# The last unit of a retention and mixture-of-adapters kernel: small products moved between engines, its copies reordered, its stores regrouped

## The chip, the cores and the metric

The kernel runs on one core of a Trainium2 chip. The metric is the device time of one execution in microseconds; runs are compared by their medians.

## The reference

Two stages, the second fed by the first. Retention over 8 batches, 8 heads, 576 positions and head dimension 64; then, for each of the 4608 tokens (512 numbers each), a mixture of 8 adapters of rank 16, of which the best two by a gate are added to the token.

```python
scores = scale * np.matmul(q, k.transpose(0, 1, 3, 2))
ret = scores * Dmat[None, :, :, :]          # Dmat: gamma_h ** (i - j) where i >= j, else 0
attn_out = np.matmul(ret, v)
x = attn_out.transpose(0, 2, 1, 3).reshape(B * S, H * D)
logits = x @ w_gate
# the two largest logits of each token, softmax over these two -> w
delta[mask] += w[mask, k, None] * (z @ B[e])   # z = x[mask] @ A[e]
return x + delta
```

## The kernel before, in words

The sequence is cut into chunks of 128 positions, and a unit is one chunk of two batches. The last 64 positions of the sequence are half a chunk, so there a unit takes four batches: rows 0 to 63 of a tile belong to two batches, rows 64 to 127 to the next two. These are the units NU-2 and NU-1, the last two of all. In their output tiles the column index `b` (0 or 1) and the row half `t` (0 or 1) together name the batch, `4*bp + 2*t + b`.

Per unit: queries and keys are scaled and transposed (`stage_T`), scores are made (`stage_S`), masked on DVE, and multiplied with the values and the running state (`stage_X`, PSUM tile `px`). The result, already transposed, is copied to SBUF as `xT`. Logits and adapter inputs come out of one product (`stage_Z`, `pz`), 128 columns of adapter inputs and 8 gate logits. The gate works on these: the two largest (`max`), a threshold test (`ge`), a sigmoid on ACT (`sg`), their product on POOL (`cm`), and the weighted adapter inputs (`zc`), also on POOL. `zc` is transposed on PE (`pzt`), copied on ACT (`zT`), and multiplied with the second adapter matrix (`stage_Y`), which adds to a PSUM tile `po` into which `stage_B` has transposed `xT` back. `evict_o` copies `po` to `osb`, and `store` sends `osb` to memory.

The program order on each engine is the order in which the code is written (a manual schedule): nothing reorders it. `finish()` writes out the end by hand. There the last unit is split by column half `b`, and its tiles carry an `e`: `pze` and `ze` (logits), `nse`, `gee`, `sge`, `cme`, `zce`, `pzte`, `zTe`, `poe`, `oe`. In the order of before, `finish()` computes both `pze` halves (L714), then for each half the gate (L726 to L740), with the small step of unit NU-2 between them; then `stage_B`, `stage_Y`, `evict_o` and `store` of unit NU-2; then the transposes and output products of the last unit (`small_b`, `output_b`).

Stores of full chunks (L525) send 128 rows of 512 numbers of one batch, 256 KB in one piece of memory. The two units of half chunks store each batch by itself, 64 rows, 128 KB in one piece of memory (L530 for unit NU-2, of which two on POOL's queue; L776 for the last unit, of which one on ACT's queue).

Of the kernel before, what the change touches and what calls it, by code (L numbers as in the profile page):

```python
# [10 lines left out]
FP32 = mybir.dt.float32  # L11
FP16 = mybir.dt.float16

ALU = mybir.AluOpType
AFT = mybir.ActivationFunctionType
# [3 lines left out]
def kernel(  # L19
# [10 lines left out]
    nc = tc.nc  # L30
    B, H, S, Dh = q.shape
    Ntok, Dm = out.shape
    E = moe_w_gate.shape[1]
    R = moe_A.shape[2]
    ER = E * R
    HP = H // 2
# [9 lines left out]
    scale = 1.0 / float(np.sqrt(Dh))  # L46
# [34 lines left out]
    mo = ctx.enter_context(tc.tile_pool(name="moe", bufs=2))  # L81
    pp = ctx.enter_context(tc.tile_pool(name="pp", bufs=1, space=bass.MemoryType.PSUM))
# [6 lines left out]
    ident16 = cpool.tile([128, 128], FP16, tag="ident16", name="ident16", align_bytes=256)  # L89
# [4 lines left out]
    id64 = pack[:, 0:64]  # L94
# [12 lines left out]
    NU = len(units)  # L107
# [267 lines left out]
    def stage_P(u, tag="x1"):  # L375
        pzt = pp.tile([128, 2, 128], FP16, tag=tag, name="pzt")
        for b in range(2):
            nc.tensor.matmul(
                pzt[:, b, :], lhsT=st[u]["zc"][:, b, :], rhs=ident16,
                is_transpose=True, start=True, stop=True,  # L380
            )
        st[u]["pzt"] = pzt

    def evict_z(u):
        zt = mo.tile([128, 2, 128], FP16, tag="zT", name="zT")
        nc.scalar.copy(out=zt, in_=st[u]["pzt"])
        st[u]["zT"] = zt
# [82 lines left out]
    def stage_Y(u):  # L470
        s = st[u]
        bv = Bcat.rearrange("p (a o d) -> p a o d", a=HP, o=2)
        for ho in range(2):
            for b in range(2):
                nc.tensor.matmul(  # L475
                    s["po"][ho][:, b, :, :],
                    lhsT=s["zT"][:, b, :],
                    rhs=bv[:, :, ho, :],
                    start=False,
                    stop=True,  # L480
                    skip_group_check=True,
                )

    def evict_o(u, engines=(nc.scalar, nc.scalar)):
        s = st[u]
        s["osb"] = mo.tile(
            [128, 2, HP, 2, 64], FP32, tag="osb", name="osb", bufs=3, align_bytes=256
        )
        for ho in range(2):
            eng = engines[ho]  # L490
            copy = eng.copy if eng is nc.scalar else eng.tensor_copy
            copy(out=s["osb"][:, :, :, ho, :], in_=s["po"][ho])  # L492
# [23 lines left out]
            )  # L516

    o3 = out.rearrange("(b s) m -> b s m", s=S)

    def store(u):  # L520
        c, bp = units[u]
        of = st.pop(u)["osb"].rearrange("p b a o d -> p b (a o d)")
        for b in range(2):
            if c < NFULL:
                nc.sync.dma_start(  # L525
                    out=o3[2 * bp + b, 128 * c : 128 * c + 128, :], in_=of[:, b]
                )
            else:
                for t in range(2):
                    (nc.gpsimd if b and u == NU - 2 else nc.sync).dma_start(  # L530
                        out=o3[4 * bp + 2 * t + b, 128 * c : 128 * c + 64, :],
                        in_=of[64 * t : 64 * t + 64, b],
                    )


    def load_batch(u, w, b):
        c, bp = units[u]
# [17 lines left out]
    for dt in range(HP):  # L555
        nc.sync.dma_start(  # L556
            out=AW[:, dt, 0:ER].rearrange("p (e r) -> p e r", e=E),
# [96 lines left out]
    def back(u):  # L654
        if has(u):
            stage_B(u)
# [6 lines left out]
    def small(u, tag="x1"):  # L663
        if has(u):
            stage_P(u, tag)
            evict_z(u)
# [26 lines left out]
    def finish():  # L693
        u = NU - 1
        s = st[u]
        store(u - 3)
        routing_4(u - 2)
        scores(u)
        logits(u - 1)
        small(u - 2)  # L700
        back(u - 2)
        choose(u - 1)
        routing_3(u - 1)
        output(u - 2)
        routing_4(u - 1)
        products(u)
        store(u - 2)

        bv = Bcat.rearrange("p (a o d) -> p a o d", a=HP, o=2)
        pz, zs, zc, po, osb = [], [], [], [], []  # L710
        for b in range(2):
            pz.append(pp.tile([128, ER + E], FP32, tag=f"u{b}", name="pze"))
            for dt in range(HP):
                nc.tensor.matmul(  # L714
                    pz[b], lhsT=s["xT"][b][:, dt, :], rhs=AW[:, dt, :],
                    start=(dt == 0), stop=(dt == HP - 1), skip_group_check=True,
                )
        for b in range(2):
            z = mo.tile([128, ER + E], FP32, tag=f"ze{b}", name="ze", bufs=1)
            m8 = mo.tile([128, E], FP32, tag=f"m8e{b}", name="m8e", bufs=1)  # L720
            ns = mo.tile([128, 1], FP32, tag=f"nse{b}", name="nse", bufs=1)
            ge = mo.tile([128, E], FP32, tag=f"gee{b}", name="gee", bufs=1)
            sg = mo.tile([128, E], FP32, tag=f"sge{b}", name="sge", bufs=1)
            cm = mo.tile([128, E], FP32, tag=f"cme{b}", name="cme", bufs=1)
            c = mo.tile([128, ER], FP16, tag=f"zce{b}", name="zce", bufs=1)
            nc.scalar.copy(out=z, in_=pz[b])  # L726
            nc.vector.max(out=m8, in_=z[:, ER : ER + E])
            nc.vector.scalar_tensor_tensor(
                out=ns, in0=m8[:, 0:1], scalar=-1.0, in1=m8[:, 1:2],
                op0=ALU.mult, op1=ALU.subtract,  # L730
            )
            nc.vector.tensor_tensor(
                out=ge, in0=z[:, ER : ER + E],
                in1=m8[:, 1:2].broadcast_to((128, E)), op=ALU.is_ge,
            )
            nc.scalar.activation(
                out=sg, in_=z[:, ER : ER + E], func=AFT.Sigmoid, bias=ns, scale=2.0
            )
            nc.gpsimd.tensor_tensor(out=cm, in0=ge, in1=sg, op=ALU.mult)
            nc.gpsimd.tensor_tensor(  # L740
                out=c.rearrange("p (e r) -> p e r", e=E),
                in0=z[:, 0:ER].rearrange("p (e r) -> p e r", e=E),
                in1=cm.unsqueeze(2).broadcast_to((128, E, R)),
                op=ALU.mult,
            )
            zc.append(c)
            if b == 0:
                small(u - 1, "x0")
        back(u - 1)
        stage_Y(u - 1)  # L750
        evict_o(u - 1, (nc.scalar, nc.vector))
        store(u - 1)

        def small_b(b):
            p = pp.tile([128, 128], FP16, tag=f"u{b}", name="pzte")
            nc.tensor.matmul(
                p, lhsT=zc[b], rhs=ident16, is_transpose=True, start=True, stop=True
            )
            zt = mo.tile([128, 128], FP16, tag=f"zTe{b}", name="zTe", bufs=1)
            nc.scalar.copy(out=zt, in_=p)  # L760
            return zt

        def output_b(b, zt):
            o = mo.tile([128, HP, 2, 64], FP32, tag=f"oe{b}", name="oe", bufs=1, align_bytes=256)
            for ho, eng in ((0, nc.scalar), (1, nc.vector)):
                nc.tensor.matmul(
                    po[b][ho], lhsT=zt, rhs=bv[:, :, ho, :],
                    start=False, stop=True, skip_group_check=True,
                )
                (eng.copy if eng is nc.scalar else eng.tensor_copy)(  # L770
                    out=o[:, :, ho, :], in_=po[b][ho]
                )
            c, qd = units[u]
            of = o.rearrange("p a o d -> p (a o d)")
            for t in range(2):
                (nc.scalar if b and t else nc.sync).dma_start(  # L776
                    out=o3[4 * qd + 2 * t + b, 128 * c : 128 * c + 64, :],
                    in_=of[64 * t : 64 * t + 64],
                )

        zt0 = small_b(0)
        for b, tag in ((0, "s"), (1, "x")):
            po.append(
                [pp.tile([128, HP, 64], FP32, tag=f"{tag}{ho}", name="poe") for ho in range(2)]
            )
            for dt in range(HP):
                for ho in range(2):
                    sl = slice(64 * ho, 64 * ho + 64)
                    nc.tensor.matmul(
                        po[b][ho][:, dt, :], lhsT=s["xT"][b][sl, dt, :], rhs=id64[sl, :],  # L790
                        is_transpose=True, start=(dt == 0), stop=False, skip_group_check=True,
                    )
        output_b(0, zt0)
        output_b(1, small_b(1))

    stage_A(2)
    logits(0)
# [103 lines left out]
```

## Time and profile before

| | us |
|---|---|
| median of 3 runs | 190.33 (190.16 to 191.59) |
| profiled execution, its time | 190.79 |
| profiled execution, its span | 188.9 |
| outside the span | 1.9 |

Engines are busy for these shares of the span: PE 89%, weight loads 79%, DVE 60%, ACT 60%, POOL 58%. Times in the timeline are microseconds from the span's start; a timeline line gives start, duration, engine, source line, operation, tiles written and read, the count, and the idle time before it with what ended it. In the DMA views, a slice digit is the mean busy share of the core's 16 DMA engines in tenths, and the line below it is the rate in GB/s. A DMA instruction on a queue (SPq, ACTq, or on POOL) is the issuing of a transfer; the transfer itself runs on the DMA engines afterwards.

### The profile page before, as it was taken

The page shows a single profiled execution, that of the slowest core. Times are in us where ns is not written, and L with a number is a line of the kernel's source. Part 1 is how long each engine was busy: PE and PEld are TensorE (multiplying, and loading weights), DVE is VectorE, ACT ScalarE, POOL GpSimd, SP SyncE. Part 2 cuts the span into 40 slices and gives each one's busy share as a digit, 9 for nine tenths or more (in the row PEclk, how much of TensorE's full clock was granted, in tenths as well). Part 3 has the DMA queues.
Part 4 walks back from the last instruction along what each step waited for, and adds up shares of the span by engine and source line. Part 5 has one row for each costly group of instructions (what it writes and reads, how often), then busy time and mean ns, then how long its engine had stood idle before and what let it go on. Part 6 is the DMA issues. An engine that isn't in the chain of part 4 may idle for free.

```text
span 188.9 us, 10441 instructions
## 1 busy us (share of the span) xinstructions
PE 167.3 (89%) x4675; PEld 148.9 (79%) x4675; DVE 113.3 (60%) x227; ACT 114.1 (60%) x255; POOL 108.7 (58%) x162
## 2 busy tenths in 40 slices
PE   3989598799889889898999999999997999999960
PEld 3578498588879788788999989899996988988840
DVE  1384837665296475748577787777594846555240
ACT  3437163735569484765767868494959394674650
POOL 1333321567769988493949586675969397520240
PEclk9999969999999999999999999999999999999998
DMA  7999969999999999999999999999998853112325
GB/s 157 248 221 225 227 70 232 202 224 246 224 228 235 262 252 277 252 260 247 241 257 246 266 232 250 221 278 226 271 206 243 181 169 115 50 68 111 115 56 166
DMA packets 108075, 38.99 MB, mean 206 GB/s; under 512 B 88768, under 2 KB 103488, under 8 KB 108032
## 3 DMA queue, kind: packets, MB, share of 16 engines
q1 hardware_dynamic: 107568, 37.71, 81.1%
q8 instruction: 36, 0.59, 1.4%
q0 software_dynamic: 240, 0.39, 1.0%
q10 hardware_dynamic: 224, 0.24, 0.5%
q14 instruction: 7, 0.06, 0.1%
HBM read 29.02 MB, written 9.44 MB: 204 GB/s over the span
## 4 chain that ended last, share of the span: by engine, by line
PE 59%; SPq 14%; issue 7%; DMA 6%; POOL 5%; DVE 4%; ACT 2%; POOLq 0%; ACTq 0%
PE px L350 15%; PE pz L393 12%; PE ps_s L269 8%; PE pu L300 6%; PE po L475 5%; PE po L459 4%; PE pt_k L215 4%; SPq L148 3%; SPq L556 3%; PE pt_q L202 3%; DMA k<-in_k_dram 3%; SPq L160 3%; DMA q<-in_q_dram 3%; POOL k L179 2%; SPq L538 2%
## 5 line engine op out<-in xcount | busy, mean ns | idle before, releaser
L179 POOL TENSOR_TENSOR k<-k,pack 128x512 f32<-128x512 f32 x32 | 34.9, 1109 | 17.4 <-DMA k<-in_k_dram 16.5
L350 PE MATMUL px<-x,v 128*64 128x64 f32 (+1 forms) x576 | 39.3, 226 | 2.6 <-DVE x L289 0.8
L289 DVE TENSOR_TENSOR x<-ps_s,pack 64x512 f32<-64x512 f32 (+1 forms) x38 | 25.1, 660 | 25.9 <-PE ps_s L269 25.6
L350 PE MATMUL px<-qT,v 128*64 128x64 f32 (+1 forms) x576 | 39.2, 226 | 1.3 <-DVE qT L289 1.1
L350 PEld LDWEIGHTS px<-x,v 128*64 128x64 f32 (+1 forms) x576 | 36.2, 140 | 4.4 <-ACT kT L240 1.0
L350 PEld LDWEIGHTS px<-qT,v 128*64 128x64 f32 (+1 forms) x576 | 36.1, 140 | 1.9 <-DVE qT L289 1.2
L393 PE MATMUL pz<-AW,xT 128*128 128x136 f32 x272 | 36.1, 286 | 0.6 <-ACT kT L240 0.6
L393 PEld LDWEIGHTS pz<-AW,xT 128*128 128x128 f32 x272 | 32.6, 190 | 1.8 <-ACT kT L240 0.8
L169 POOL TENSOR_TENSOR qs<-q,pack 128x512 f32<-128x512 f32 x25 | 26.1, 1062 | 4.1 <-DMA q<-in_q_dram 4.1
L406 ACT COPY zs<-pz 128x272 f32<-128x272 f32 x17 | 6.6, 386 | 33.2 <-PE pz L393 32.5
L289 DVE TENSOR_TENSOR qT<-ps_s,pack 64x512 f32<-64x512 f32 (+1 forms) x38 | 25.1, 660 | 1.1
L269 PE MATMUL ps_s<-qT,kT 64*64 64x64 f32 x1152 | 23.6, 224 | 2.1 <-issue 1.4
L269 PEld LDWEIGHTS ps_s<-qT,kT 64*64 64x64 f32 x1152 | 20.4, 137 | 6.2 <-issue 3.1
L441 POOL TENSOR_TENSOR cm<-ge,sg 128x16 f32<-128x16 f32 x17 | 4.0, 234 | 36.5 <-PE pt_k L215 16.9
L316 POOL COPY v<-SP 64x512 f32<-64x512 f32 x32 | 20.5, 640 | 1.6
L300 PE MATMUL pu<-v,k 64*64 64x64 f32 x1024 | 19.2, 221 | 0.8 <-DMA v<-in_v_dram 0.8
L240 ACT COPY kT<-pt_k 128x512 f32<-128x512 f32 x34 | 18.2, 589 | 1.2 <-PE pt_k L215 1.0
L253 DVE COPY x<-qT 64x512 f32<-64x512 f32 x17 | 14.5, 852 | 7.4 <-ACT qT L235 5.0
L366 ACT COPY xT<-px 128x512 f32<-128x512 f32 x28 | 16.3, 625 | 4.4 <-PE px L350 4.4
L300 PEld LDWEIGHTS pu<-v,k 64*64 64x64 f32 x1024 | 16.9, 134 | 2.5 <-DMA v<-in_v_dram 0.9
L492 ACT COPY osb<-po 128x512 f32<-128x512 f32 x33 | 17.6, 584 | 1.0 <-PE po L475 1.0
L252 DVE COPY x<-qT 64x512 f32<-64x512 f32 x14 | 8.1, 579 | 16.0 <-ACT qT L235 12.0
(68 smaller groups left out, 242.6 us busy)
## 6 DMA issues: line engine op xcount, KB each, us to landing
v<-in_v_dram SPq DMA_DIRECT2D x36, 256.0 KB, 5.2
q<-in_q_dram SPq DMA_DIRECT2D x34, 256.0 KB, 5.2
out_dram<-osb SPq DMA_DIRECT2D x32, 256.0 KB, 4.2
k<-in_k_dram SPq DMA_DIRECT2D x15, 512.0 KB, 5.7
k<-in_k_dram SPq DMA_DIRECT2D x6, 256.0 KB, 4.3
q<-in_q_dram SPq DMA_DIRECT2D x1, 512.0 KB, 6.9
out_dram<-oe SPq DMA_DIRECT2D x3, 128.0 KB, 3.3
AW<-in_moe_A_dram SPq DMA_DIRECT2D x4, 64.0 KB, 3.6
```

Of the source, the lines that this page charges most:

```text
L169: engines[b].tensor_tensor(out=qs[:, :, 4 * b : 4 * b + 4, :].rearrange("p e h d -> p h e d"), in0=tl[:, b * H : b * H + H, :].rearrange(" ...
L179: engines[b].tensor_tensor(out=tl[:, b * H : b * H + H, :], in0=tl[:, b * H : b * H + H, :], in1=g[:, c, :].unsqueeze(2).broadcast_to((128 ...
L240: nc.scalar.copy(out=tl[:, r], in_=st[u]["p" + w][r])
L253: eng.tensor_copy(out=x2[0:64, 1, b], in_=qT[64:128, 1, b])
L269: nc.tensor.matmul(ps[ho][64 * t : 64 * t + 64, b, hp, :], lhsT=kT[sl, t, b, hp, :], rhs=qT[sl, t, b, hp, :], start=(hp == 0 and b == bs[0 ...
L289: nc.vector.tensor_tensor(out=out, in0=in0, in1=m, op=ALU.mult)
L300: nc.tensor.matmul(pu[t][64 * ho : 64 * ho + 64, b, hp, :], lhsT=kn[sl, h, :], rhs=block(u, t)[sl, h, :], start=(hp == 0 and b == 0), stop ...
L316: copy(out=dst[:, :, :, ho, :], in_=src[64 * ho : 64 * ho + 64])
L350: nc.tensor.matmul(px[b][64 * ho : 64 * ho + 64, hp, t, :], lhsT=block(u, t)[rw, b * H + 2 * hp + ho, :], rhs=facing(u, t, ho)[rw, b, hp, ...
L366: nc.scalar.copy(out=xt.rearrange("p a (t i e) -> p (a t) e i", t=2, e=2), in_=px.rearrange("p a t (e i) -> p (a t) e i", e=2),)
L393: nc.tensor.matmul(pz[:, b, :], lhsT=st[u]["xT"][b][:, dt, :], rhs=AW[:, dt, :], start=(dt == 0), stop=(dt == HP - 1), skip_group_check=True,)
L492: copy(out=s["osb"][:, :, :, ho, :], in_=s["po"][ho])
```

## The change

Only `finish()` and the branch of `store` that serves the half chunks are touched.

1. In the last unit, `cm` and `zc` are computed on DVE in place of POOL.
2. The last unit's second logits copy (`ze` of half 1) and its `max`, `nse`, `gee` are issued ahead of unit NU-2's `zT` copy.
3. `stage_B` of the last unit's half 0 comes before `stage_Y` of unit NU-2; the last unit's output copies are all on ACT; both output copies of unit NU-2 go to DVE, behind the last unit's second `zc`; the store of unit NU-2 is issued after the last unit's first store.
4. Each column half `b` of these two units is stored as one transfer from 128 partitions. In memory it is two runs of 64 rows, one for each batch `t`, with other batches between them. The store of unit NU-2 is two transfers on SP; the last unit's first is on SP, its second on ACT.

```diff
     o3 = out.rearrange("(b s) m -> b s m", s=S)
+    o5 = out.rearrange("(g t b s) m -> g b t s m", t=2, b=2, s=S)
...
             else:
-                for t in range(2):
-                    (nc.gpsimd if b and u == NU - 2 else nc.sync).dma_start(
-                        out=o3[4 * bp + 2 * t + b, 128 * c : 128 * c + 64, :],
-                        in_=of[64 * t : 64 * t + 64, b],
-                    )
-
+                nc.sync.dma_start(
+                    out=o5[bp, b, :, 128 * c : 128 * c + 64, :], in_=of[:, b]
+                )
...
+        def choose_b(b):
+            z, m8 = small_tile("ze", b, ER + E), small_tile("m8e", b, E)
+            ns, ge = small_tile("nse", b, 1), small_tile("gee", b, E)
             nc.scalar.copy(out=z, in_=pz[b])
             nc.vector.max(out=m8, in_=z[:, ER : ER + E])
...
+        def sigmoid_b(b):
+            sg = small_tile("sge", b, E)
             nc.scalar.activation(
-                out=sg, in_=z[:, ER : ER + E], func=AFT.Sigmoid, bias=ns, scale=2.0
-            )
-            nc.gpsimd.tensor_tensor(out=cm, in0=ge, in1=sg, op=ALU.mult)
-            nc.gpsimd.tensor_tensor(
+                out=sg, in_=ze[b][:, ER : ER + E], func=AFT.Sigmoid, bias=nse[b], scale=2.0
+            )
...
+        def weigh_b(b):
+            cm, c = small_tile("cme", b, E), small_tile("zce", b, ER, FP16)
+            nc.vector.tensor_tensor(out=cm, in0=gee[b], in1=sge[b], op=ALU.mult)
+            nc.vector.tensor_tensor(
                 out=c.rearrange("p (e r) -> p e r", e=E),
...
             p = pp.tile([128, 128], FP16, tag=f"u{b}", name="pzte")
...
+            zt = small_tile("zTe", b, 128, FP16)
             nc.scalar.copy(out=zt, in_=p)
             return zt
...
+        def back_b(b, tag):
...
+        def output_b(b, zt, engines):
...
+            (nc.scalar if b else nc.sync).dma_start(
+                out=o5[qd, b, :, 128 * c : 128 * c + 64, :],
+                in_=o.rearrange("p a o d -> p (a o d)"),
+            )
+
+        choose_b(0)
+        sigmoid_b(0)
+        stage_P(u - 1, "x0")
+        choose_b(1)
+        evict_z(u - 1)
+        back(u - 1)
+        back_b(0, "s")
+        zt0 = weigh_b(0)
+        stage_Y(u - 1)
+        sigmoid_b(1)
+        back_b(1, "x")
+        output_b(0, zt0, (nc.scalar, nc.scalar))
+        zt1 = weigh_b(1)
+        evict_o(u - 1, (nc.vector, nc.vector))
+        store(u - 1)
+        output_b(1, zt1, (nc.scalar, nc.scalar))
```

More of the change, by code (lines that the diff above doesn't have):

```diff
@@ L709, in finish @@
         bv = Bcat.rearrange("p (a o d) -> p a o d", a=HP, o=2)
-        pz, zs, zc, po, osb = [], [], [], [], []
+        pz, po = [], []
         for b in range(2):
@@ L717, in finish, with small_tile @@
                 )
[L718 to L725, printed above, removed]
+        def small_tile(name, b, n, dt=FP32):
+            return mo.tile([128, n], dt, tag=f"{name}{b}", name=name, bufs=1)
+        ze, nse, gee, sge = [], [], [], []
+        def choose_b(b):
+            z, m8 = small_tile("ze", b, ER + E), small_tile("m8e", b, E)
+            ns, ge = small_tile("nse", b, 1), small_tile("gee", b, E)
             nc.scalar.copy(out=z, in_=pz[b])
@@ L735, in finish @@
             )
+            ze.append(z), nse.append(ns), gee.append(ge)
+        def sigmoid_b(b):
+            sg = small_tile("sge", b, E)
             nc.scalar.activation(
-                out=sg, in_=z[:, ER : ER + E], func=AFT.Sigmoid, bias=ns, scale=2.0
+                out=sg, in_=ze[b][:, ER : ER + E], func=AFT.Sigmoid, bias=nse[b], scale=2.0
             )
-            nc.gpsimd.tensor_tensor(out=cm, in0=ge, in1=sg, op=ALU.mult)
-            nc.gpsimd.tensor_tensor(
+            sge.append(sg)
+        def weigh_b(b):
+            cm, c = small_tile("cme", b, E), small_tile("zce", b, ER, FP16)
+            nc.vector.tensor_tensor(out=cm, in0=gee[b], in1=sge[b], op=ALU.mult)
+            nc.vector.tensor_tensor(
                 out=c.rearrange("p (e r) -> p e r", e=E),
-                in0=z[:, 0:ER].rearrange("p (e r) -> p e r", e=E),
+                in0=ze[b][:, 0:ER].rearrange("p (e r) -> p e r", e=E),
                 in1=cm.unsqueeze(2).broadcast_to((128, E, R)),
@@ L745, in finish @@
             )
[L746 to L754, printed above, removed]
             p = pp.tile([128, 128], FP16, tag=f"u{b}", name="pzte")
             nc.tensor.matmul(
-                p, lhsT=zc[b], rhs=ident16, is_transpose=True, start=True, stop=True
+                p, lhsT=c, rhs=ident16, is_transpose=True, start=True, stop=True
             )
-            zt = mo.tile([128, 128], FP16, tag=f"zTe{b}", name="zTe", bufs=1)
+            zt = small_tile("zTe", b, 128, FP16)
             nc.scalar.copy(out=zt, in_=p)
             return zt
-        def output_b(b, zt):
+        def back_b(b, tag):
+            ps = [pp.tile([128, HP, 64], FP32, tag=f"{tag}{ho}", name="poe") for ho in range(2)]
+            for dt in range(HP):
+                for ho in range(2):
+                    sl = slice(64 * ho, 64 * ho + 64)
+                    nc.tensor.matmul(
+                        ps[ho][:, dt, :], lhsT=s["xT"][b][sl, dt, :], rhs=id64[sl, :],
+                        is_transpose=True, start=(dt == 0), stop=False, skip_group_check=True,
+                    )
+            po.append(ps)
+        def output_b(b, zt, engines):
             o = mo.tile([128, HP, 2, 64], FP32, tag=f"oe{b}", name="oe", bufs=1, align_bytes=256)
-            for ho, eng in ((0, nc.scalar), (1, nc.vector)):
+            for ho, eng in enumerate(engines):
                 nc.tensor.matmul(
@@ L773, in output_b @@
             c, qd = units[u]
[L774 to L778, printed above, removed]
-                )
[L781 to L784, printed above, removed]
-            )
[L786 to L794, printed above, removed]
+            (nc.scalar if b else nc.sync).dma_start(
+                out=o5[qd, b, :, 128 * c : 128 * c + 64, :],
+                in_=o.rearrange("p a o d -> p (a o d)"),
+            )
+        choose_b(0)
[14 more added lines that the diff above has]
+        output_b(1, zt1, (nc.scalar, nc.scalar))
     stage_A(2)
```

## The prediction

> **What bounds the end now.** The diff touches only what runs after about 178.7 us. I read the timeline of that stretch engine by engine, then the waits of the SP queue, then the DMA view, because the last thing that happens is a store. ACT and DVE, then the queues:
>
> ```profile
> 179.46 0.30 ACT L736 ACTIVATE sge<-ze,nse 128x8 f32<-128x8 f32 x1 [0.49 <-DVE gee L732]
> 179.73 0.37 ACT L386 COPY zT<-pzt 128x256 f16<-128x256 f16 x1
> 180.00 0.28 ACT L726 COPY ze<-pze 128x136 f32<-128x136 f32 x1
> 181.44 0.27 ACT L760 COPY zTe<-pzte 128x128 f16<-128x128 f16 x1
> 182.08 0.37 ACT L770 COPY oe<-poe 128x256 f32<-128x256 f32 x1 [0.38 <-PE poe L766]
> 182.35 0.27 ACT L760 COPY zTe<-pzte 128x128 f16<-128x128 f16 x1
> 183.62 0.56 ACTq L776 DMA_DIRECT2D out_dram<-oe  x1
> ...
> 180.59 0.16 DVE L732 TENSOR_TENSOR gee<-ze,m8e 128x8 f32<-128x8 f32 x1
> 180.91 0.69 DVE L492 COPY osb<-po 128x512 f32<-128x512 f32 x1 [0.17 <-PE po L475]
> 182.19 0.42 DVE L770 COPY oe<-poe 128x256 f32<-128x256 f32 x1 [0.59 <-PE poe L766]
> 183.10 0.42 DVE L770 COPY oe<-poe 128x256 f32<-128x256 f32 x1 [0.49 <-PE poe L766]
> ...
> 181.67 1.18 SPq L530 DMA_DIRECT2D out_dram<-osb  x2
> 182.96 2.25 SPq L776 DMA_DIRECT2D out_dram<-oe  x3
> ...
> SPq L896 <- DMA out_dram<-oe: 2.4, 1, 2.4
> ```
>
> All arithmetic is over at 183.52 (183.10 + 0.42), 5.4 us before the span ends at 188.9. The last store is issued by SP, done at 185.21 (182.96 + 2.25), and is waited for another 2.4 us. The DMA view of 182.5 to 187.5 us, in slices of 0.125 us, shows the transfers of the two last units:
>
> ```profile
> DMA  0026999428979927899979668698998789853000
> GB/s 0 0 49 180 246 246 180 115 66 197 279 197 246 295 98 246 279 443 246 344 230 295 246 213 295 230 344 279 328 311 213 180 295 344 295 197 115 16 16 0
> DMA packets 576, 1.05 MB, mean 210 GB/s; under 512 B 128, under 2 KB 128, under 8 KB 576
> ```
>
> Their 1.05 MB flow from about 182.8 to 187.1 us, 4.3 us at 245 GB/s, with all engines mostly busy; 1.8 us follow until the end of the span. So the end hangs on the output transfers, and their pace is what I price first.
>
> For that, a cleaner stretch: two full-chunk stores of 256 KB by themselves, issued from 176.94 us (busy tenths of 177.5 to 179.3 us in slices of 0.045 us and its packets, then two half microseconds with the DMA share and GB/s in the last columns):
>
> ```profile
> 176.94 0.81 SPq L525 DMA_DIRECT2D out_dram<-osb  x2
> ...
> DMA  0000007599799979799799999799899959751000
> DMA packets 288, 0.52 MB, mean 291 GB/s; under 512 B 32, under 2 KB 32, under 8 KB 288
> q1 hardware_dynamic: 288, 0.52, 75.8%
> ...
> 178.00:178.50 0.50, 0.50 (x7) 0.50 (x6) 0.00 (x0) 0.14 (x1) 0.00 (x0) 1.00 1.04 397
> 178.50:179.00 0.50, 0.50 (x7) 0.50 (x6) 0.01 (x1) 0.27 (x1) 0.00 (x0) 1.00 1.07 414
> ```
>
> Two things are to be seen. The 288 packets are 256 rows of 2 KB and 32 small ones, 16 for each transfer; in the end stretch above it is again 128 small ones for 8 transfers. So each transfer is spread over all 16 engines, and each engine closes its share with one small packet. And with all 16 at work (share 1.04 to 1.07), the rate is 397 to 414 GB/s, mean 405, or 25.3 GB/s for each engine.
>
> **The change, part by part.** First the regrouped stores, because they decide. Every transfer of this kernel before has on both sides a pattern whose outermost count is 64 or 128: rows of SBUF partitions on one side, positions or one contiguous piece of memory on the other. 64 and 128 divide by 16. The new transfers have 128 partitions on one side, and on the memory side two runs that can't be merged, because other batches lie between them: outermost count 2. An instruction that hands out shares to the engines by the outermost loop of both patterns can then make only two shares. The trace holds no such transfer, so I bound it: if it still spreads over 16 engines, 256 KB take 0.65 us (262 KB at 405 GB/s); if two engines carry it, 5.2 us each (262 KB at 2 x 25.3 = 50.6 GB/s). I take two engines: what all the transfers in the trace with 16 small packets have in common is an outer count that 16 divides, and the new pattern loses exactly that.
>
> [...]
>
> If two engines carry each transfer and the shares are handed out from the first engine on, all four transfers queue on the same two. The sum of data is unchanged, 1.05 MB, so the stage takes 1049 KB / 50.6 GB/s = 20.7 us in place of 4.3. For the bounds of the pace of an engine on its own: fastest, the single best 0.125 us slice of the end stretch, 443 GB/s, is 27.7 GB/s an engine, hence 18.9 us; slowest, the pace under mixed queues in the same stretch:
>
> ```profile
> q1 hardware_dynamic: 400, 0.66, 42.7%
> q0 software_dynamic: 96, 0.26, 22.9%
> q10 hardware_dynamic: 80, 0.13, 8.4%
> ```
>
> These shares sum to 74.0% of 16 engines over 5 us, 59.2 engine-us for 1.05 MB, 17.7 GB/s, hence 29.6 us. The quiet stretch has 21.8 engine-us (75.8% of 16 x 1.8) for 524 KB, 24.0 GB/s, hence 21.8 us. With nothing else running the quiet stretch is the nearest row, so 20.7 stands.
>
> Next, when the flow starts. I walk the chain with the durations above.
>
> - Logits ahead. ACT takes `ze` of half 1 at 179.73 and `zT` at 180.00, swapped. `zT` is late by 0.27 us, and with it `stage_Y` of unit NU-2, but PE has the moved transposes of half 0 to do meanwhile:
>
> ```profile
> 179.62 0.71 PE L459 MATMUL po<-pack,xT 64*128 64x64 f32 x16
> 180.26 0.61 PE L475 MATMUL po<-Bcat,zT 128*128 128x256 f16 x4
> 180.86 0.71 PE L789 MATMUL poe<-pack,xT 64*128 64x64 f32 x16
> 181.76 0.39 PE L766 MATMUL poe<-Bcat,zTe 128*128 128x256 f16 x2 [0.18 <-ACT zTe L760]
> ...
> 180.12 0.40 POOL L740 TENSOR_TENSOR zce<-ze,cme 128x128 f16<-128x128 f32 x1
> 182.20 1.12 POOL L530 DMA_DIRECT2D out_dram<-osb  x2 [0.37 <-issue]
> ```
>
>   They run from 180.26 to 180.92, so the swap costs nothing; without that cover it would cost 0.27.
> - Weights on DVE. `cm` costs 0.16 there (the 128x8 `gee`); `zc`, 128x128, lies between 0.16 and 0.42 (the 128x256 copy), I take 0.27, against 0.40 on POOL. DVE does the second half's `max`, `nse`, `gee` first, until about 180.5, so `zc` of half 0 is ready near 180.87, later than POOL's 180.52; the transposes on PE end at 180.92 and hide it. A cost of up to 0.15 is left if `zc` takes 0.42.
> - Half 0. `pzte` runs at 180.92, `zTe` on ACT from 181.17 to 181.44, PE has `stage_Y` and the half-1 transposes until 182.2, then the two output products. Two copies on ACT, 0.32 after the first product starts (182.08 after 181.76) and 0.27 apart (182.35 after 182.08), end at about 183.15. In before the same tile was whole at 182.61 (182.19 + 0.42, the DVE copy). SP issues at about 183.3.
> - Half 1. The sigmoid waits on ACT behind `zTe` of half 0, until 181.75; `zc` of half 1 is ready at 182.25; `zTe` of half 1 waits behind both output copies, until 183.35; the output copies end at about 184.35, and ACT issues from 184.45, done near 185.0. This is 0.8 later than ACT's issue before, and just ahead of SP's last one (185.21).
> - Unit NU-2. Its two output copies on DVE come behind `zc` of half 1, 182.25 to 183.6 (2 x 0.69). Their stores stand on SP behind that of half 0 (183.3), which costs them nothing as they are ready later; they are issued near 183.8 and 184.4. POOL's two issues (1.12 us) and SP's other two are gone; they were beside the flow and are worth nothing by themselves.
>
> Data follow an issue by 0.83 us in the quiet stretch (176.94 to 177.77) and by 1.1 at 181.67; with 1.0, the flow starts at 184.3 in place of 182.8. The stores were split over three queues and began early; now they begin 1.5 us later.
>
> **The sum.** 184.3 + 20.7 + 1.8 = 206.8 us of span, 17.9 more than 188.9. With the 1.9 us outside the span, 208.7 for an execution like the profiled one (190.79). That one stands 0.46 above the median of 190.33, so 208.2 for the median.
>
> **The rivals.**
>
> 1. *All 16 engines still carry each transfer.* For it: every transfer of the trace does, row by row, and a row of 2 KB is its unit on both sides. Against it: the memory side's outer loop has two steps. The flow starts at 184.3, the last issue ends at 185.0, 1.05 MB take between 2.6 us (405 GB/s) and 4.3 us (245); the last quarter can't be there before 185.0 + 0.5 + 0.65 = 186.1. The end of the flow is 186.9 to 188.6, against 187.1 now: 190.1 to 191.8, I take 190.5. This is the case that is not slower; below 2.6 us of data the place where it decides is the issue on ACT. [...] 8 in 100.
> 2. *Two engines for each transfer, but another pair each time.* Then the four run beside each other. The last one starts flowing at 184.45 + 1.0 and takes 5.2: 190.65, which is 3.55 after 187.1, so 193.9. For it: nothing in the trace shows which engines a small share takes. 5 in 100.
> 3. *Two engines that work at the pace of the mixed stretch*, 17.7 GB/s each, two queues (SP and ACT) taking turns on them: 29.6 us in place of 20.7, so 217.1. For it: the end of before, also from several queues, ran at that pace; against it: only the last of four transfers comes from another queue. 5 in 100.
>
> The forecast, two engines in common at about 25 GB/s, has 82 in 100. The range is 204 to 213: its lower end is below the forecast with 27.7 GB/s (206.4) by 2.4, for a start that is earlier and a lighter-loaded engine that may be quicker than its sixteenth of a full stream; its upper end is the forecast at 20.8 GB/s, halfway between 24.0 and 17.7 (25.2 us, so 212.7). The three rivals lie outside. One percent, 1.9 us, is about what a measurement of this kernel can tell from no change. Rival 1 gives 7 in 100 within it and 1 faster by more; all else is slower: 92 in 100.
>
> **What would show it.** If I am right, the DMA share after 184.3 us is about 0.13 (2 of 16) for some 20 us at about 50 GB/s, the four last transfers post 2 small packets each in place of 16, every engine is idle, and SP waits nearly 20 us for the last landing. The last landing comes from unit NU-2's second store or the last unit's second one. The swap is right if the second `max` on DVE starts near 180.05 in place of 180.31, and `zc` near 0.27 us. A DMA share near 1 and an end at 189 would prove the first step wrong, a share of 0.25 to 0.5 the common pair, and 0.13 at 35 GB/s the pace.

## The result and the profile after

The changed kernel takes 209.99 us (median of four runs, 208.63 to 210.75) beside 190.67 us: a ratio of 1.0999 with a 95% interval from 1.0926 to 1.1073. Some executions of any of these kernels fall into a slower group, so ratios here and below compare the faster executions alone and can differ from the ratio of the medians shown. The profiled execution took 209.83 us, its span is 207.8 us.

The DMA view of the changed kernel from 182.5 us to the end of its span, in slices of 0.63 us, answers to the view of the last transfers shown of before. The lines are the busy tenths of the 16 engines, GB/s, packets, and the two queues.

```profile
DMA  0001111111111111111111111111111111111100
GB/s 0 0 0 23 29 26 26 39 36 49 52 52 52 52 52 52 52 52 49 49 52 52 52 52 52 52 52 52 49 49 52 52 52 52 52 52 52 45 0 0
DMA packets 520, 1.05 MB, mean 41 GB/s; under 512 B 8, under 2 KB 8, under 8 KB 520
q1 hardware_dynamic: 390, 0.79, 8.7%
q10 hardware_dynamic: 130, 0.26, 2.7%
```

The same 1.05 MB flow, but by the packet records from 184.47 to 206.54 us, 22.1 us; the records of before give 182.87 to 187.35, 4.5 us, of which the last 0.3 are single rows. The 520 packets are 512 rows and 8 small ones: 2 for each of the four transfers, where before had 16. The windows view gives the share of the 16 engines and the rate in its last two columns:

```profile
184.50:188.50 4.00, 0.00 (x0) 0.00 (x0) 0.00 (x0) 0.00 (x0) 0.00 (x0) 0.83 0.13 31
188.50:206.00 17.50, 0.00 (x0) 0.00 (x0) 0.00 (x0) 0.00 (x0) 0.00 (x0) 0.50 0.13 51
```

A share of 0.13 is two engines of 16. It stays there from the first transfer to the last, also while several transfers are pending. The busy columns of all engines are zero; the 0.83 and 0.50 before the share are the granted TensorE clock. The waits of SP and the queues' timeline show the same from the issuing side:

```profile
SPq L904 <- DMA out_dram<-osb: 13.5, 2, 8.5
SPq L904 <- DMA out_dram<-oe: 3.5, 1, 3.5
...
183.21 0.66 SPq L782 DMA_DIRECT2D out_dram<-oe  x1
183.97 5.67 SPq L530 DMA_DIRECT2D out_dram<-osb  x2
184.40 1.15 ACTq L782 DMA_DIRECT2D out_dram<-oe  x1
...
184.56 5.09 SPq L530 DMA_DIRECT2D out_dram<-osb  x1
```

The last line is the second of the two issues of the line above by itself. SP has issued its last store at 189.64 (183.97 + 5.67); this second issue alone held the queue for 5.1 us, and after that SP waits 17 us for landings. No further transfer stands behind it and the two engines stay busy meanwhile (share 0.13), so the blocked issue itself costs nothing here.

The compute of the tail, ACT and DVE of the changed kernel:

```profile
179.06 0.27 ACT L724 COPY ze<-pze 128x136 f32<-128x136 f32 x1 [0.54 <-PE pze L712]
180.03 0.25 ACT L724 COPY ze<-pze 128x136 f32<-128x136 f32 x1
180.18 0.37 ACT L386 COPY zT<-pzt 128x256 f16<-128x256 f16 x1
182.53 0.65 ACT L778 COPY oe<-poe 128x256 f32<-128x256 f32 x2 [0.58 <-PE poe L774]
183.73 0.65 ACT L778 COPY oe<-poe 128x256 f32<-128x256 f32 x2 [0.38 <-PE poe L774]
...
180.32 0.17 DVE L725 MAX8 m8e<-ze 128x8 f32<-128x8 f32 x1 [0.51 <-ACT ze L724]
180.87 0.29 DVE L746 TENSOR_TENSOR zce<-ze,cme 128x128 f16<-128x128 f32 x1
182.55 1.29 DVE L492 COPY osb<-po 128x512 f32<-128x512 f32 x2
```

All arithmetic ends at 184.38. The first row is the landmark for what follows: the first `ze` copy is the first instruction on ACT that belongs to the edited part, and what lies ahead of it is the same in all kernels, except that the kernels called interleaved below write four of the `xT` copies in another pattern. In before it starts here:

```profile
178.69 0.27 ACT L726 COPY ze<-pze 128x136 f32<-128x136 f32 x1 [0.55 <-PE pze L714]
```

So the end stretch, from this copy to the end of the span, is 188.9 - 178.69 = 10.2 us before and 207.8 - 179.06 = 28.7 us after. Of the 18.9 us that the span is longer, 18.5 lie there and 0.4 ahead of it.

### The profile page after: what moved, and what is told of

Read it like the earlier page. It is cut to its first block, busy times and chain, and to the rows that moved or that the text cites. A ratio compares the mean times of both kernels' runs of the same rounds, so it can differ in the third digit from the quotient of the medians.

```text
span 207.8 us, 10431 instructions
## 1 busy us (share of the span) xinstructions
PE 166.9 (80%) x4675; PEld 148.6 (71%) x4675; DVE 114.8 (55%) x230; ACT 113.7 (55%) x256; POOL 106.0 (51%) x156
## 4 chain that ended last, share of the span: by engine, by line
PE 53%; SPq 12%; issue 7%; POOL 5%; DMA 5%; DVE 4%; ACT 2%; POOLq 0%; ACTq 0%
PE px L350 14%; PE pz L393 11%; PE ps_s L269 8%; PE pu L300 6%; PE po L475 4%; PE pt_k L215 4%; PE po L459 3%; SPq L148 3%; PE pt_q L202 3%; SPq L554 3%; DMA k<-in_k_dram 2%; DMA q<-in_q_dram 2%; SPq L160 2%; POOL k L179 2%; SPq L536 2%
## 5 line engine op out<-in xcount | busy, mean ns | idle before, releaser
L350 PE MATMUL px<-x,v 128*64 128x64 f32 (+1 forms) x576 | 38.8, 225 | 2.3 <-ACT kT L240 0.9
L350 PE MATMUL px<-qT,v 128*64 128x64 f32 (+1 forms) x576 | 38.6, 225 | 1.1 <-DVE qT L289 1.1
L316 POOL COPY v<-SP 64x512 f32<-64x512 f32 x32 | 19.9, 621 | 1.6
L253 DVE COPY x<-qT 64x512 f32<-64x512 f32 x17 | 15.3, 897 | 7.8 <-ACT qT L235 5.3
L240 ACT COPY kT<-pt_k 128x512 f32<-128x512 f32 x34 | 18.2, 588 | 1.5 <-PE pt_k L215 1.3
L492 ACT COPY osb<-po 128x512 f32<-128x512 f32 x32 | 17.0, 585 | 0.7 <-PE po L475 0.6
L215 PE MATMUL pt_k<-pack,k 64*128 64x64 f32 x288 | 15.0, 239 | 2.7 <-DVE k L179 2.1
```

The lines of the kernel that those rows point to most:

```text
L215: nc.tensor.matmul(ps[r][:, b, hp, :], lhsT=src[sl, b * H + 2 * hp : b * H + 2 * hp + 2, :], rhs=id64[sl, :], is_transpose=True, start=Tru ...
L240: nc.scalar.copy(out=tl[:, r], in_=st[u]["p" + w][r])
L316: copy(out=dst[:, :, :, ho, :], in_=src[64 * ho : 64 * ho + 64])
L350: nc.tensor.matmul(px[b][64 * ho : 64 * ho + 64, hp, t, :], lhsT=block(u, t)[rw, b * H + 2 * hp + ho, :], rhs=facing(u, t, ho)[rw, b, hp, ...
```

## The experiments

The part ahead of the `ze` copy moves by some microseconds from one execution to the next: the kernel before had medians of 194.0 to 194.4 us beside these experiments. Totals are therefore given as ratios to before on the same chip, and the end stretch is compared besides. It is read from one profiled execution of each kernel; the one kernel that was profiled twice, before with interleaved rows, gave 8.37 and 8.36 us. The totals that were expected were worked out against 190.7, so those measured lie some 3.5 us higher throughout, three of them above the range expected (order only, stores only, pieces of 32 and 32 rows).

| kernel | end stretch, us | ratio to before (95%) |
|---|---|---|
| before | 10.2 | 1 |
| changed | 28.7 | 1.100 (1.093 to 1.107) |
| order only | 10.9 | 1.012 (1.004 to 1.020) |
| stores only | 27.7 | 1.100 (1.085 to 1.115) |
| pieces of 62 and 2 rows | 28.1 | 1.092 (1.078 to 1.105) |
| pieces of 32 and 32 rows | 11.5 | 1.018 (1.008 to 1.028) |
| changed, rows interleaved | 9.6 | 1.000 (0.995 to 1.005) |
| before, rows interleaved | 8.4 | 0.998 (0.993 to 1.003), again 0.988 (0.981 to 0.994) |
| pieces of 61 and 3 rows | 46.3 | 1.188 (1.179 to 1.197) |
| changed, half of the data in two-run transfers | 20.1 | 1.056 (1.047 to 1.065) |

**Which part of the change.** First the change with the stores of before, then the stores of the change in the order of before.

```diff
-                nc.sync.dma_start(
-                    out=o5[bp, b, :, 128 * c : 128 * c + 64, :], in_=of[:, b]
-                )
+                for t in range(2):
+                    (nc.gpsimd if b and u == NU - 2 else nc.sync).dma_start(
+                        out=o3[4 * bp + 2 * t + b, 128 * c : 128 * c + 64, :],
+                        in_=of[64 * t : 64 * t + 64, b],
+                    )
```

(and the same for the last unit, with its fourth transfer on ACT).

> The changed kernel in all but its stores: each column half is stored again as two transfers of 64 rows, on the queues of before. Theory (the count of two on the memory side decides, two of 16 engines carry the data): the whole loss goes away, small closing packets are 16 per transfer again, the DMA share near 1 again; the flow of 1.05 MB starts 1.5 us later than before but compute and issues end at about the same time, so 190.5, between 189.5 and 192.5. Rival (the later order of copies and stores is what costs): it stays near 205 to 210.

Measured: 195.07 us beside 194.22, an end stretch of 10.9 us. The total lies 2.6 us above the range of the expectation, which was worked out against a before 3.5 us faster; in the end stretch, the only part that the edit touches, the order alone costs 0.7 us.

The other way round, from the kernel before:

```diff
+    o5 = out.rearrange("(g t b s) m -> g b t s m", t=2, b=2, s=S)
...
-                for t in range(2):
-                    (nc.gpsimd if b and u == NU - 2 else nc.sync).dma_start(
...
+                nc.sync.dma_start(
+                    out=o5[bp, b, :, 128 * c : 128 * c + 64, :], in_=of[:, b]
+                )
...
+            (nc.scalar if b else nc.sync).dma_start(
+                out=o5[qd, b, :, 128 * c : 128 * c + 64, :],
```

> The kernel before with only its stores regrouped: one transfer of two runs for each column half (three on SP, one on ACT), everything else as before. Theory (two engines carry all four): the flow starts 1.5 us sooner than in the changed kernel, near 183.0, and takes 20.7 to 22.0 us, so 207.0 to 209.0, 2 small packets per transfer. Rival (the order): within 1% of before, about 190.7.

Measured: 212.54 us, an end stretch of 27.7 us, 17.5 more than before. The two parts add up: 0.7 + 17.5 = 18.2 of the 18.5 us. The stores carry the loss.

**Two runs of memory, or a count of two.** A store of 64 rows is one run of memory. Cut into 62 and 2 rows, each piece still is, but 16 divides neither 62 nor 2, as it does 64 and 128; 2 divides both. The control has pieces of 32 and 32 rows.

```diff
                 for t in range(2):
+                    for r0, r1 in ((0, 62), (62, 64)):
...
-                        out=o3[4 * bp + 2 * t + b, 128 * c : 128 * c + 64, :],
-                        in_=of[64 * t : 64 * t + 64, b],
+                        out=o3[4 * bp + 2 * t + b, 128 * c + r0 : 128 * c + r1, :],
+                        in_=of[64 * t + r0 : 64 * t + r1, b],
```

(and the same for the last unit; in both kernels POOL issues none of these stores.)

> The kernel before, each store of 64 rows cut into pieces of 62 and 2 rows, all on SP and ACT: every piece is one run of memory, nothing is strided. Theory as a divisor rule (the largest number up to 16 that divides the outermost count: 62 and 2 both give 2): again two engines carry everything, 2 small packets per transfer, 207 to 211. Rival (what costs are the two separate runs of memory): 16 engines, and only the issues count: SP issues 12 transfers at 0.55 us from 181.7 to 188.3, landing 2.4 later, so 193.4.

> Control for the number of transfers: as the 62 and 2 rows, but each store cut into 32 and 32. Both theories: 16 engines, 16 small packets per transfer; SP issues 12 transfers of about 0.55 us from 181.7 to 188.3, landing 2.4 later, so about 193.4 (192 to 195).

Measured: 210.65 us and 28.1 us of end stretch for 62 and 2 rows, 196.31 us and 11.5 us for 32 and 32, with equally many transfers. The packets of the two, first 62 and 2, then 32 and 32 (whose view also holds the two full-chunk stores ahead):

```profile
DMA packets 544, 1.05 MB, mean 40 GB/s; under 512 B 32, under 2 KB 32, under 8 KB 544
...
DMA packets 1056, 1.57 MB, mean 123 GB/s; under 512 B 288, under 2 KB 288, under 8 KB 1056
```

32 small packets for 16 transfers are 2 each; 288 for 18 transfers are 16 each. So it is not the strided memory that costs, but the count: the same loss comes without any second run (28.1 us of end stretch, 27.7 with two runs). A prime count puts the same theory to a sharper test; only the numbers of the diff change, 62 to 61.

> The kernel before, each store of 64 rows cut into 61 and 3 rows, each one run of memory, on SP and ACT. Theory as a divisor rule: 61 is prime, so one engine carries 61 rows of each 64, 3 engines the rest; 1.0 MB on one engine at 25.5 GB/s is 39 us, DMA share 0.06: from the first ze copy to the end about 46 us (44 to 49), total near 226. Rival (an uneven count costs a little, rows are dealt out nearly evenly): as the 32 and 32 rows, 11.5 us from the first ze copy. Rival 2 (the engines of small shares rotate from one transfer to the next): 8 transfers on 8 engines at 4.9 us each, near 15.

Measured: 230.52 us, an end stretch of 46.3 us, as expected. The windows view of this kernel shows one engine of 16 at work (0.07), at the same pace per engine:

```profile
190.00:200.00 10.00, 0.00 (x0) 0.00 (x0) 0.00 (x0) 0.00 (x0) 0.00 (x0) 0.50 0.07 26
200.00:210.00 10.00, 0.00 (x0) 0.00 (x0) 0.00 (x0) 0.00 (x0) 0.00 (x0) 0.50 0.07 26
```

The eight transfers of 61 rows run one after the other on one engine at 26 GB/s: the small shares do not rotate.

**The same two runs on 16 engines.** If partition 2i + t holds position i of batch t, the memory pattern of a column half can be written with 64 positions outermost and the two batches inside. The copy that writes `xT` does the interleaving at no extra instruction; the mean of the eight copies of its line, four of which are interleaved, goes from 592 to 615 ns.

```diff
-                nc.scalar.copy(out=xt, in_=px.rearrange("p a t i -> p a (t i)"))
+                dst = xt.rearrange("p a (t i) -> p a t i", t=2)
+                if units[u][0] == NFULL:
+                    dst = xt.rearrange("p a (i t) -> p a t i", t=2)
+                nc.scalar.copy(out=dst, in_=px)
...
-    o5 = out.rearrange("(g t b s) m -> g b t s m", t=2, b=2, s=S)
+    o6 = out.rearrange("(g t b s) m -> g b s t m", t=2, b=2, s=S)
...
-                    out=o5[bp, b, :, 128 * c : 128 * c + 64, :], in_=of[:, b]
+                    out=o6[bp, b, 128 * c : 128 * c + 64], in_=of[:, b]
```

(and the same for the last unit's two stores.)

> The changed kernel with the rows of the two half-chunk units interleaved in SBUF (partition 2i + t holds position i of batch t, done by the copy that writes xT), so that each column half is still one transfer of 256 KB to the same two runs of memory, but with 64 positions outermost in place of 2 runs. Theory (the outermost count decides): 16 engines, 16 small packets per transfer, the whole loss gone; from the first ze copy to the end of the span 9.5 to 10.5 us in place of 28.7 (before: 10.2), so within 1% of before. Rival (two separate runs in one transfer are slow in themselves): it stays near 28 us, ratio 1.09 to 1.10.

Measured: ratio 1.000 (0.995 to 1.005), an end stretch of 9.6 us. Two half microseconds from the middle of its transfers show all engines at the pace of the quiet stretch of before:

```profile
189.50:190.00 0.50, 0.00 (x0) 0.00 (x0) 0.00 (x0) 0.00 (x0) 0.00 (x0) 1.00 1.04 397
190.00:190.50 0.50, 0.00 (x0) 0.00 (x0) 0.00 (x0) 0.00 (x0) 0.00 (x0) 1.00 1.06 414
```

Number of transfers, bytes, queues and the memory written are those of the changed kernel; only the order of the rows within a transfer differs, and with it the outermost count, and some 19 us go with it.

> The kernel before with the same interleaved rows: four stores of 256 KB over 16 engines in place of eight of 128 KB. Theory: issues on SP take 0.35 to 0.45 us each for three transfers, flow from 182.7 at up to 405 GB/s, the last quarter (ACT's, issued at 183.6) done at 185.4 in place of 187.1: from the first ze copy to the end 8.5 to 9.2 us in place of 10.2, 0.5 to 0.9% faster than before. Rival (two separate runs are slow in themselves): near 27.7 as with the two-run stores in the order of before.

Measured: an end stretch of 8.4 us, a little better than expected, but the total was not told apart from before (0.998, 0.993 to 1.003). It was timed again:

> The kernel before with interleaved rows and four stores of 256 KB, timed in more rounds. Theory: what was saved behind the first ze copy (8.4 us in place of 10.2) shows in the total, 0.5 to 1.2% faster than before. Rival: the earlier end is offset by something ahead of it (the xT copies with a stride), and the total is within 0.3% of before.

Measured: 191.43 us beside 194.03, ratio 0.988 (0.981 to 0.994), an end stretch of 8.4 us once more. In the second timing this version is faster than before, in the first it could not be told apart; the end stretch was 1.8 us shorter, 0.9% of the total, both times. Its DMA view in slices of 0.14 us, from 183.0 us to the end:

```profile
GB/s 0 0 0 0 0 0 0 0 0 0 102 439 410 366 410 425 380 410 424 351 381 439 439 366 322 366 395 439 439 190 0 0 0 0 0 0 0 0 0 0
DMA packets 576, 1.05 MB, mean 187 GB/s; under 512 B 64, under 2 KB 64, under 8 KB 576
```

That view is of its first run. The 1.05 MB take 2.8 us in place of 4.5: four transfers on two queues run at 320 to 440 GB/s without a gap, where eight on three queues had 234 on average. Whether the number of transfers or the missing third queue (POOL's) did this was not taken apart.

**Whether the engines are common.** In the changed kernel, unit NU-2 is stored as before (the first diff of this section alone, without the last unit's), the last unit as changed.

> The changed kernel, but unit NU-2 stored as before in transfers of 64 rows; only the last unit's two transfers have two runs. Theory (two common engines, time as bytes on them): 512 KB at 51 GB/s is 10.3 us, with 64 KB more of unit NU-2's share on these two engines 11.5, and the slow first 4 us as seen (1.3 more): from the first ze copy to the end 18.4 to 20 us. Rival (each transfer has its own pair): 13 to 15 us.

Measured: 205.10 us, an end stretch of 20.1 us, just above the 20 expected and far from the rival's 15. The stores of unit NU-2, which are spread over 16 engines and landed after 2.3 and 3.0 us in before, now land late. The view of this kernel counts 68 small packets, 4 x 16 for these stores and 2 x 2 for the last unit's, so each store of unit NU-2 is still spread over 16 engines and has a share on the two that the last unit's transfers fill:

```profile
out_dram<-osb SPq DMA_DIRECT2D x2, 128.0 KB, 9.6
out_dram<-osb POOLq DMA_DIRECT2D x2, 128.0 KB, 7.5
```

**The parts in engine order.** Each is one edit of the interleaved kernel in the order of before, run once, so only its end stretch is compared.

```diff
-            nc.gpsimd.tensor_tensor(out=cm, in0=ge, in1=sg, op=ALU.mult)
-            nc.gpsimd.tensor_tensor(
+            nc.vector.tensor_tensor(out=cm, in0=ge, in1=sg, op=ALU.mult)
+            nc.vector.tensor_tensor(
                 out=c.rearrange("p (e r) -> p e r", e=E),
```

> As the interleaved kernel in the order of before, with cm and zc of the last unit on DVE in place of POOL, nothing else moved. Theory: zc takes 0.29 on DVE against 0.40 on POOL, but DVE's copy of unit NU-2's output then stands behind zc of half 1 and the first stores are issued 0.5 to 0.7 us later; from the first ze copy to the end 8.8 to 9.2 us in place of 8.4. Rival (a shorter zc comes out at the end): 8.2 or less.

Measured: 9.15 us from the `ze` copy to the end, 0.8 more. DVE's copy of unit NU-2's output comes right behind `zc`:

```profile
185.16 0.29 DVE L741 TENSOR_TENSOR zce<-ze,cme 128x128 f16<-128x128 f32 x1
185.53 0.69 DVE L495 COPY osb<-po 128x512 f32<-128x512 f32 x1
```

It starts 2.98 us after this kernel's `ze` copy (182.55), in place of 2.22 on the kernel without this edit.

```diff
             nc.scalar.copy(out=z, in_=pz[b])
+            if b == 1:
+                evict_z(u - 1)
...
             if b == 0:
-                small(u - 1, "x0")
+                stage_P(u - 1, "x0")
```

> As the interleaved kernel in the order of before, with the last unit's second logits copy ahead of unit NU-2's zT copy, nothing else moved. Theory: half 1's gate is done about 0.3 us earlier, but its zTe copy still stands behind half 0's output copy on ACT, so from the first ze copy to the end 8.3 to 8.5 us, unchanged. Rival: the 0.3 us come out at the end, 8.1.

Measured: 8.31 us, unchanged as expected, but not for the reason given there: the last output copy does end 0.14 us earlier, 4.70 in place of 4.84 us after the `ze` copy. What did not move is the first store. Below is that issue in the interleaved kernel in the order of before, with this edit, and in the interleaved kernel in the changed order:

```profile
183.21 1.27 SPq L533 DMA_DIRECT2D out_dram<-osb  x2
...
184.26 1.27 SPq L533 DMA_DIRECT2D out_dram<-osb  x2
...
187.29 0.62 SPq L785 DMA_DIRECT2D out_dram<-oe  x1
```

From the `ze` copy these are 2.98, 2.97 and 4.15 us, and 3.73 with the weights on DVE. In all four kernels the end comes 5.3 to 5.4 us after this first issue (end stretches 8.4, 8.3, 9.6 and 9.15), and in the DMA views of two of them, those without a further edit, in the order of before and in the changed order, the data flow behind it without a gap (318 to 439 GB/s in every full slice); so the first store, not the last, sets the end.

## Why the prediction was right

The forecast was 208.2 us with a range of 204 to 213; measured were 209.99. Its steps, one by one:

- *The outermost count of two leaves two engines.* Right: 2 small packets per transfer, a share of 0.13. The experiments turn this from a reading of the code into a shown cause: a count of 2 without a second run costs as much (28.1 us of end stretch for 62 and 2 rows, 27.7 for the stores only), a count of 61 twice as much (46.3), and the same two runs with 64 outermost nothing (9.6 beside 28.7). The divisor rule of the expectations was put as a theory; it fits the counts that ran, 128, 64, 32, 62, 61, 3 and 2 (the run with 61 and 3 rows has 32 small packets, as 8 x 1 and 8 x 3 give), and no run shows another. One transfer of 128 partitions in place of two of 64 paid only with the outermost count kept: 8.4 us with interleaved rows, 27.7 with two runs, beside 10.2 before.
- *All four transfers share the same two.* Right: 51 GB/s in all, also while SP's and ACT's transfers run side by side, and the late landings of unit NU-2 in the mixed kernel (9.6 and 7.5 us in place of 2.3 and 3.0). That the shares are handed out from the first engine on was the author's assumption; no view tells which two engines they are. Rival 2 had 193.9.
- *20.7 us for the data.* Mis-sized by 1.4 us: it took 22.1. The steady pace, 51 GB/s, is the 50.6 of the forecast, but for the first 4 us it was 31, which is 15.5 per engine. Rival 3's pace, 17.7 GB/s per engine throughout, did not come, though SP's and ACT's rows took turns later on.
- *The flow starts at 184.3.* Right within 0.2: counted from the `ze` copy, 5.4 us in place of the 5.6 forecast. Three terms in it were wrong and nearly cancelled. I took all 16 transposes of `xT` (0.66 us) for one half, which has 8:

```profile
180.54 0.41 PE L765 MATMUL poe<-pack,xT 64*128 64x64 f32 x8
181.22 0.23 PE L753 MATMUL pzte<-ident,zce 128*128 128x128 f16 x1 [0.26 <-DVE zce L746]
```

  So PE was free sooner and had to wait 0.26 us for `zc`, a wait which I had put down as hidden. The transposes of half 1 were counted too long as well, and with them SP's first issue came 0.46 us earlier than I had it (4.15 us after the `ze` copy, forecast 4.61). Against that, the data followed this issue by 1.26 us where I took 1.0.
- *The swap of the logits copy.* Right: the second `max` starts 1.26 us after the first `ze` copy in place of 1.62 (180.31 - 178.69 in before), and the edit alone leaves the end where it was. The 0.27 us that it was to cost without cover did not come: run alone, without the moved transposes, it has `zT` done only 0.09 us later, and unit NU-2's output copy on DVE, which waits for `stage_Y`, starts 2.22 us after the `ze` copy with and without it.
- *Weights on DVE.* `zc` took 0.29 us, forecast 0.27. That unit NU-2's output copies wait behind it was priced at nothing for the new order, and no run takes that apart; in the order of before it costs 0.8 us.
- *1.8 us after the last data.* It was 1.3 (207.84 - 206.54). The 1.8 was counted from 187.1, while the view of before shows single rows until about 187.3; from there it is 1.5.
- *The step to the median.* The profiled execution stood 0.46 above the median before; after, it stands 0.16 below. Of the 1.8 us that the forecast is low, 0.6 are this, 0.6 the end stretch (28.7 in place of 28.1), 0.4 lie ahead of the edited part, 0.1 outside the span.

Rival 1, a kernel near 190 us, is what the change would have been with 64 outermost: its interleaved form came out level with before. Of the 1.8 us that the four interleaved stores gain in the end stretch, the order costs 1.2: 9.6 us with it, 8.4 without, as the first store is issued 1.2 us later.

## What to carry to other kernels

Before two transfers are merged into one, write down the outermost count of both patterns as the instruction will carry them, on the memory side too; here counts of 32 and 64 kept 16 engines (16 small packets for each transfer), 2 and 62 left two (about 51 GB/s) and 61 left one (26 GB/s), for the whole transfer, and the transfers then queued on the same few. If the batches must be the outer stride in memory, put the rows outermost in the pattern and interleave them in SBUF where a copy runs anyway; here this brought the end stretch from 28.7 to 9.6 us. To see in a trace how many engines a transfer had, count its small closing packets (16 or 2 here), or read the DMA share while nothing else flows (1.04, 0.13 and 0.07 here).

## What the runs showed of the hardware that was not expected

- With two engines the flow began slowly, 31 GB/s in the first 4 us and 51 after. In the changed kernel, the packet records of the first 3.5 us show the rows two at a time and, after the first few, in groups of four, three of 84 ns and one of 149 to 382 ns; after that rows take 84 ns, one every 80 ns on each engine (25.6 GB/s). With one engine (61 and 3 rows) the DMA view has 15 GB/s in the first two slices of the flow, 2.2 us, and 24 to 30 after; with 16 engines (interleaved rows) the flow is at 403 and 439 GB/s in its second slice, of 0.17 and 0.14 us. Why is open: no run here took it apart.
- An issue can be held long: the third two-run transfer on SP's queue held it 5.1 us in the changed kernel and 4.8 us with the stores only, against 0.55 to 0.62 for SP's last stores in the interleaved kernels. Issues of full-chunk stores, over 16 engines, took up to 2.7 us earlier in the program of the changed kernel. What an issue waits for is open.
